# Decayed attention and two MLPs on one core: loads paced by the landing of earlier loads, in place of TensorE products behind instruction-block borders

## The chip, the core and the metric

The kernel runs on one core of one Trainium2 chip. A core has a matrix engine (TensorE, in the profile PE for the products and PEld for the loading of weights into its array), VectorE (DVE), ScalarE (ACT), GpSimd (POOL) and SyncE (SP), which here does nothing but issue transfers. Sixteen DMA engines move the data. The metric is the device time of one execution in microseconds. Before the change it is 558.35 us, the median of three runs (558.33 to 558.46).

## The reference

Three stages follow one another: a blockwise attention with decay over 2 batches, 8 heads, 768 positions and 64 features, then two MLPs over 1536 tokens, 512 features and 2048 hidden features. All of it is in float32.

```python
for b in range(nb):                       # 12 blocks of 64 positions
    qb, kb, vb = (q[:, :, sl], k[:, :, sl], v[:, :, sl])
    intra = einsum('bhic,bhjc->bhij', qb, kb) * Dmask
    intra = einsum('bhij,bhjd->bhid', intra, vb)
    inter = einsum('bhid,bhde->bhie', qb * lam_pow, kv_state)
    out[:, :, sl] = intra + inter
    kv_state = lam_block * kv_state + einsum('bhsd,bhse->bhde', kb * rev_pow, vb)
...
h = x @ w_in;  x = (h * clip(h + 3, 0, 6) / 6) @ w_out      # first MLP
h = x @ w_in2; x = maximum(0.01 * h, h) @ w_out2            # second MLP
```

## The kernel before

**The work.** The attention goes through 12 chunks of 64 positions, both batches at once. For a chunk c, TensorE makes three groups of small float32 products: `scores(c)` (tile `pair`), `state(c)` (tile `a`) and `attn_out(c)` (tile `h`). Around them ScalarE copies the queries (`queries`, L314), the states (`state_copy`, L336) and the high part of the result (`att_x`, L353); VectorE masks the scores (`mask`, L322) and makes the low part (L351); GpSimd decays the keys (`k_decay`, L296). ScalarE and VectorE share the copies of v (`part_v`, L289). The MLPs follow; each weight slice is loaded as `raw`, taken apart by `low_bits` (L416), `magnitude` (L420), `exponent` and `compose`, and split into a high and a low part (`w_high` L445, `w_low` L449), so that a product is three faster ones. The first products of the first MLP (`gemm1(0)`, from the first slice, called w(0,0,0) here) are laid between the last chunks of the attention.

**The loads.** All inputs come through SP's queue, in the order of `LOAD_ORDER` (L47). A chunk's q and k are three loads of 256 KB, the v of two chunks are two loads, and the first weight slices are two loads each. Numbered from 0, load 15 is the last of chunk 3, loads 16 to 18 are chunk 4, 19 and 20 are v of chunks 4 and 5, 21 to 26 are chunks 5 and 6, 27 and 28 v of 6 and 7, 29 to 31 chunk 7, 32 and 33 w(0,0,0), 34 to 36 chunk 8, 37 and 38 v of 8 and 9, 39 to 44 chunks 9 and 10, 45 and 46 v of 10 and 11, 47 and 48 w(0,0,1), 49 to 51 chunk 11. Four buffers hold q and k, three hold v, three hold raw weights.

**The pacing of the loads.** TensorE's program is cut in blocks of 256 instructions, the first border at instruction 193. `mm` counts the instructions and notes the first product at least 8 behind each border. From load 15 on, each group of six loads waits for such a product (`load`, L153 on): loads 15 to 20 for the first border's, 21 to 26 for the second's, and so on.

**The order of the work.** `Order` is a planner. Every operation has engines, a planned duration, a due time, predecessors, and buffers that it takes and frees. `issue` (L69 on) runs a clock of its own, and whenever an engine is free in that clock it issues the ready operation that is due first. Each engine's program is the order in which that happened; on the chip, each engine runs its program strictly in order. The loads take part as operations of one planned engine, "dma" (2.05 for a chunk's three loads, 1.4 for the two of v, 1.45 for a weight slice, and 2.5 more until the data count as there). `in_order` makes each load follow the one before it in `LOAD_ORDER`, and makes the first of a group of six follow the attention product named for it in `AT_BORDER`. These planned times are not times of the chip; they set the order only.

Of the kernel before, what the change touches and what calls it, by code (L numbers as in the profile page):

```python
# [9 lines left out]
F32 = mybir.dt.float32  # L10
# [30 lines left out]
N_DENSE = {("s", 0): 5}  # L41
NQ = 4

FIRST_BORDER, BLOCK, PAST_BORDER = 193, 256, 8
FIRST_LOADS, LOADS_PER_BLOCK = 15, 6
AT_BORDER = (('o', 0), ('o', 1), ('s', 4), ('t', 4), ('o', 5), ('s', 8), ('t', 8), ('o', 9))
LOAD_ORDER = (('qk', 0), ('v', 0), ('qk', 1), ('qk', 2), ('v', 2), ('qk', 3), ('qk', 4), ('v', 4), ('qk', 5), ('qk', 6), ('v', 6), ('qk', 7), (0, 0, 0), ('qk', 8), ('v', 8), ('qk', 9), ('qk', 10), ('v', 10), (0, 0, 1), ('qk', 11))  # L47


class Order:  # L50
# [7 lines left out]
    def add(self, engines, fn, due=1e9, after=(), takes=(), frees=()):  # L58


        engines = [engines] if isinstance(engines, tuple) else engines
        self.ops.append((engines, fn, due, [a for a in after if a is not None], list(takes), list(frees)))
        return len(self.ops) - 1
# [59 lines left out]
def decay_attention_two_mlps(ctx: ExitStack, tc: tile.TileContext, qkk, vv, lam, w1, w2, out):  # L123
    nc = tc.nc
# [13 lines left out]
    od = Order({**sizes, "q": NQ, "pair": 2, **{n: 0 for n in late}, **{f"acc{e}": 0 for e in range(4)}})  # L138
    add = od.add

    def new(n, shape, dtype, name=None):
        return pool[n].tile(shape, dtype, tag=name or n, name=name or n)


    records, borders, loads = [0], [], []

    def mm(out, a, x, **flags):
        at = FIRST_BORDER + BLOCK * len(borders) + PAST_BORDER
        i = nc.tensor.matmul(out, a, x, **flags)  # L149
        if records[0] >= at:  # L150
            borders.append(i.ins)
        records[0] += 4 if a.dtype == F32 else 2

    def load(out, in_):
        i = nc.sync.dma_start(out=out, in_=in_)  # L155
        k = (len(loads) - FIRST_LOADS) // LOADS_PER_BLOCK
        loads.append(i)
        if 0 <= k < len(AT_BORDER):
            tc.add_manual_dep(i.ins, borders[min(k, len(borders) - 1)].name, mybir.DependencyInfo(
                mybir.DependencyClass.Sync, mybir.DependencyReason.DATA), reason="behind the border")  # L160

    starts = [[sum(bs[:i]) for i in range(len(bs) + 1)] for bs in BLOCKS]
    steps = [(l, b, t, f) for l in range(2) for b in range(len(BLOCKS[l])) for t in range(NTT)
# [36 lines left out]
    def dense(n):  # L200

        for i in range(n):
            mm(PA["warm"], zeros[:, :P], zeros.unsqueeze(1).to_broadcast([P, 2, TT // 2]), start=True,
                             stop=True)
# [24 lines left out]
    def lam_rows(_):  # L229

        PA["lam"] = new("h", [P, H], F32)
        mm(PA["lam"], ones, lam_sb, start=True, stop=True)
# [36 lines left out]
    def load_qk(c):  # L269
        def fn(_):  # L270
            for i in (0, 2, 1):
                load(QK[c % NQ][:, i], qkk[c, :, i])
        return fn

    def load_v(c):

        def fn(_):
            vp = new("vs", [P, 2, 2, H, D], F32)
            VS[c], VS[c + 1] = vp[:, 0], vp[:, 1]
            for i in range(2):  # L280
                load(vp[:, i, 0], vv[c + i])
            if c == 0:
                nc.gpsimd.memset(vp[other[1], 0, 1], 0.0)
        return fn
# [15 lines left out]
    def scores(c):  # L300
        def fn(_):

            ps, qk = PA["s", c], QK[c % NQ]
            for h in range(H):
                for b in range(2):
                    mm(ps[own[b], b, h, :], qk[other[b], 1, h, :], qk[other[b], 0, h, :],
                                     start=True, stop=True)
        return fn
# [29 lines left out]
    def attn_out(c):  # L338
        def fn(_):
            ps = PA["o", c] = new("h", [P, KC, 2, C], F32)  # L340
            for b in range(2):
                for h in range(H):
                    mm(ps[own[h % 2], h // 2, b, :], VS[c][:, b, h, :], R[c][:, b, h, :],
                                     start=True, stop=True)
        return fn
# [17 lines left out]
    pieces = {}  # L363
    st, copies, masks, dense_ops, att_ops = {}, {-1: []}, [], [op_warm], []
    for c in range(NSC):
# [5 lines left out]
        s = pieces["s", c] = add(pe, scores(c), d, after=[qc, op_warm])  # L371
# [10 lines left out]
        o = pieces["o", c] = add(pe, attn_out(c), d + 2.6, after=[m, ld["v", c]] + copies[c - 1], takes=["h"])  # L382
        add(("none", 0.0), nothing, after=[o, st.get(c)], frees=["vs"] * (c % 2) + ["r"])
        for n, a in (("s", s), ("t", st.get(c)), ("o", o)):
            i = N_DENSE.get((n, c), 0)
# [17 lines left out]
    def load_w(h):  # L403
        def fn(_):
            l, f, j = h
            RAW[h] = new("raw", [P, DM, 2], U32)
            raw, w = RAW[h].rearrange("p n t -> p (n t)"), (w1, w2)[l][f, j].bitcast(U32)
            for a in (slice(0, DM), slice(DM, 2 * DM)) if l + f < 2 else (slice(0, 2 * DM),):
                (load if h in LOAD_ORDER else nc.sync.dma_start)(raw[:, a], w[:, a])
        return fn  # L410

    def low_bits(h):
        def fn(_):

            CV[h] = [new("cv", [P, DM], U32, "t"), new("cl", [P, DM], U32, "c")]
            nc.scalar.activation(out=CV[h][1], in_=RAW[h][:, :, 0], func=AF.Copy, scale=2.0 ** -29)  # L416
        return fn
# [4 lines left out]
    def exponent(h):  # L422
        def fn(_):
            t = CV[h][0]

            nc.vector.tensor_scalar(out=t.bitcast(F32), in0=t.bitcast(F32), scalar1=MAG_MIN, scalar2=MAG_MAX,  # L426
                                    op0=ALU.max, op1=ALU.min)

            nc.vector.tensor_scalar(out=t, in0=t, scalar1=5, scalar2=2,
                                    op0=ALU.logical_shift_left, op1=ALU.logical_shift_right)  # L430
        return fn
# [22 lines left out]
    def w_sum(l, p, i):  # L454
        def fn(e):
            t1, t2, raw = (x.bitcast(F32) for x in (CV[l, 2 * p, 0][0], CV[l, 2 * p + 1, 0][0], RAW[l, 2 * p + 1, 0]))
            out = raw.rearrange("p n t -> p (n t)").rearrange("p (i n) -> p i n", i=4)
            k1, k2 = slice(0, 2 * P), slice(2 * P, 4 * P)
            a, b, op = ((t2[:, k1], t2[:, k2], ALU.add), (out[:, 0], t1[:, k1], ALU.subtract),
                        (t1[:, k1], t2[:, k1], ALU.subtract), (t1[:, k2], out[:, 1], ALU.subtract))[i]  # L460
            eng[e].tensor_tensor(out=out[:, i], in0=a, in1=b, op=op)
            SB[l, p, "f"] = out
        return fn
# [12 lines left out]
    for l in range(2):  # L476
        for f in range(NF):
            for j in range(2):
                h = (l, f, j)
                held = paired(l, f) and j == 0  # L480
                ld_w = ld[h] = add(("dma", 1.45), load_w(h), takes=["raw"])
                a = add(("act", 0.67), low_bits(h), after=[ld_w], takes=["cv", "cl"])
                m = add(("act", 0.67), magnitude(h), after=[ld_w, a])
                x = add(("dve", 1.2 if h in LOAD_ORDER else 0.85), exponent(h), after=[m])
# [4 lines left out]
            if paired(l, f) and f % 2:  # L489
                p, i = f // 2, None  # L490
                for n in range(4):
                    i = add(("dve", 0.43), w_sum(l, p, n), after=[composed[l, f - 1, 0], composed[l, f, 0], i])
# [3 lines left out]


    def in_order(names):
        n, behind = 0, None
        for h in names:  # L500
            op = ld["vp" if h[0] == "v" else "qk", h[1]] if len(h) == 2 else ld[h]
            k = (n - FIRST_LOADS) // LOADS_PER_BLOCK
            od.ops[op][3].extend(([pieces[AT_BORDER[k]]] if 0 <= k < len(AT_BORDER) else []) + [behind] * (behind is not None))
            n += 3 if h[0] == "qk" else 2
            behind = op
        for h in ld:
            if len(h) == 3 and h not in names:
                od.ops[ld[h]][3].append(behind)

    in_order(LOAD_ORDER)  # L510

    PH, U, G, ACC = {}, {}, {}, {}
# [311 lines left out]
    at = T_FIRST + T_STEP * n1 - 5.44  # L824
# [26 lines left out]
    for s in range(n1 - 2, NS):  # L851
        l, b, t, f = steps[s]
# [304 lines left out]
```

## Time and profile before

| what | us |
|---|---|
| median of the runs | 558.35 |
| the profiled execution, first to last instruction | 559.4 |
| TensorE products busy | 547.4 |
| VectorE busy | 431.6 |
| ScalarE busy | 361.2 |
| attention, until its last product | about 61 |

The profiled execution is 1.05 us longer than the median of the runs, so differences are worked out in the profile and then taken off the median. The page gives each engine's busy time; the table of waits tells, for each engine, what it sat idle for; the timeline lists instructions in order, with the idle time ahead of them; the table of DMA queues counts packets per queue. Queue q8, "instruction", brings TensorE's own instructions; q1 brings the loads.

### The profile page before, as it was taken

The page shows a single profiled execution, that of the slowest core. Times are in us where ns is not written, and L with a number is a line of the kernel's source. Part 1 is how long each engine was busy: PE and PEld are TensorE (multiplying, and loading weights), DVE is VectorE, ACT ScalarE, POOL GpSimd, SP SyncE. Part 2 cuts the span into 40 slices and gives each one's busy share as a digit, 9 for nine tenths or more (in the row PEclk, how much of TensorE's full clock was granted, in tenths as well). Part 3 has the DMA queues.
Part 4 walks back from the last instruction along what each step waited for, and adds up shares of the span by engine and source line. Part 5 has one row for each costly group of instructions (what it writes and reads, how often), then busy time and mean ns, then how long its engine had stood idle before and what let it go on. Part 6 is the DMA issues. An engine that isn't in the chain of part 4 may idle for free.

```text
span 559.4 us, 9243 instructions
## 1 busy us (share of the span) xinstructions
PE 547.4 (98%) x3584; PEld 462.1 (83%) x3584; DVE 431.6 (77%) x718; ACT 361.2 (65%) x634; POOL 59.7 (11%) x68
## 2 busy tenths in 40 slices
PE   8889999999999999999999999999999999999997
PEld 4788888888888888888888888888888888888885
DVE  6769999889898996878879798886467964784342
ACT  4888975668666763588668797587257744573220
POOL 6552001101101101101000000000110100110000
PEclk9999999999999999999999999999999999999999
DMA  8896325237165514334110221332332522411314
GB/s 282 268 328 222 107 87 127 39 98 204 44 164 145 138 24 109 79 110 112 51 65 0 81 108 39 113 117 72 76 76 84 143 75 45 107 43 33 76 44 108
DMA packets 24302, 59.32 MB, mean 106 GB/s; under 512 B 2882, under 2 KB 3138, under 8 KB 24258
## 3 DMA queue, kind: packets, MB, share of 16 engines
q1 hardware_dynamic: 18672, 48.77, 26.6%
q0 software_dynamic: 5184, 9.44, 10.1%
q8 instruction: 28, 0.46, 0.3%
q10 hardware_dynamic: 402, 0.52, 0.3%
q14 instruction: 16, 0.13, 0.1%
HBM read 46.14 MB, written 3.15 MB: 88 GB/s over the span
## 4 chain that ended last, share of the span: by engine, by line
PE 93%; ACT 2%; DMA 2%; issue 1%; DVE 1%; SPq 0%; ACTq 0%
PE acc L149 46%; PE h L149 28%; PE a L149 18%; DMA sums<-qkk 2%; PE pair L149 1%; ACT vs L336 1%; ACT pair L314 1%; DVE kd L251 0%; ACT xh L353 0%; DVE r L322 0%; ACT vs L289 0%; SPq L155 0%; DVE sums L1065 0%; DVE xl L351 0%; ACT t L420 0%
## 5 line engine op out<-in xcount | busy, mean ns | idle before, releaser
L568 POOL DMA_DIRECT2D sums<-st x36 | 31.8, 929 | 424.9 <-ACT st L624 408.0
L149 PE MATMUL acc<-Gh,wh 128*128 128x512 f32 x136 | 53.2, 391 | 0.0
L149 PE MATMUL acc<-Gl,wh 128*128 128x512 f32 x136 | 53.1, 390 | 0.0
L149 PE MATMUL acc<-Gh,wl 128*128 128x512 f32 x136 | 52.9, 389 | 0.0
L149 PE MATMUL acc<-wl,Gh 128*128 128x512 f32 (+1 forms) x128 | 49.6, 387 | 0.0
L149 PE MATMUL acc<-wh,Gh 128*128 128x512 f32 (+1 forms) x128 | 49.6, 387 | 0.0
L149 PE MATMUL acc<-wh,Gl 128*128 128x512 f32 (+1 forms) x128 | 49.4, 386 | 0.0
L416 ACT ACTIVATE c<-raw 128x512 uint32<-128x512 uint32 x64 | 43.0, 674 | 7.7 <-DVE t L439 5.1
L439 DVE CUSTOM_DVE_ANT_0 t<-t,c 128x1024 uint16<-128x1024 uint16 x64 | 44.3, 692 | 2.2
L626 DVE TENSOR_TENSOR sums<-acc,sums 128x512 f32<-128x512 f32 x35 | 24.1, 690 | 28.3 <-PE acc L149 28.1
L437 DVE SCALAR_TENSOR_TENSOR t<-raw,t 128x512 uint32<-128x512 uint32 x64 | 44.8, 700 | 1.0
L449 DVE TENSOR_TENSOR wl<-t,wh 128x512 fp32r<-128x512 f32 (+1 forms) x64 | 42.3, 664 | 3.0 <-ACT wh L445 2.9
L420 ACT ACTIVATE t<-raw 128x512 f32<-128x512 f32 x64 | 42.7, 666 | 0.0
L445 ACT CAST wh<-t 128x512 fp32r<-128x512 f32 (+1 forms) x64 | 37.8, 592 | 3.0 <-PE acc L149 2.3
L149 PE MATMUL h<-xh,s 128*128 128x512 f32 x112 | 38.4, 389 | 0.0
L426 DVE TENSOR_SCALAR t<-t 128x512 f32<-128x512 f32 x64 | 27.7, 433 | 12.9 <-ACT t L420 12.9
L554 DVE TENSOR_TENSOR Gl<-u,Gh 128x512 fp32r<-128x512 f32 x32 | 22.1, 689 | 17.9 <-ACT Gh L751 17.5
L757 ACT ACTIVATE u<-a 128x512 f32<-128x512 f32 x24 | 14.4, 598 | 29.1 <-PE a L149 29.1
L624 ACT COPY st<-acc 128x512 f32<-128x512 f32 x34 | 19.9, 586 | 18.8 <-PE acc L149 16.2
L149 PE MATMUL a<-xh,wl 128*128 128x256 f32 (+1 forms) x92 | 30.7, 333 | 0.0
L149 PE MATMUL a<-xl,wh 128*128 128x256 f32 (+1 forms) x92 | 30.7, 333 | 0.0
L149 PE MATMUL a<-xh,wh 128*128 128x256 f32 (+1 forms) x92 | 30.6, 333 | 0.0
(175 smaller groups left out, 1484.1 us busy)
## 6 DMA issues: line engine op xcount, KB each, us to landing
raw<-w SPq DMA_DIRECT2D x58, 512.0 KB, 3.3
sums<-qkk SPq DMA_DIRECT2D x36, 256.0 KB, 5.2
sums<-st POOLq DMA_DIRECT2D x36, 256.0 KB, 3.8
vs<-vv SPq DMA_DIRECT2D x12, 256.0 KB, 4.7
raw<-w SPq DMA_DIRECT2D x12, 256.0 KB, 4.2
out<-sums SPq DMA_DIRECT2D x19, 128.0 KB, 2.4
out<-sums ACTq DMA_DIRECT2D x3, 128.0 KB, 2.7
out<-sums SPq DMA_DIRECT2D x2, 64.0 KB, 2.3
```

The lines of the kernel that those rows point to most:

```text
L149: i = nc.tensor.matmul(out, a, x, **flags)
L416: nc.scalar.activation(out=CV[h][1], in_=RAW[h][:, :, 0], func=AF.Copy, scale=2.0 ** -29)
L420: return lambda _: nc.scalar.activation(out=CV[h][0].bitcast(F32), in_=RAW[h][:, :, 1].bitcast(F32), func=AF.Abs)
L426: nc.vector.tensor_scalar(out=t.bitcast(F32), in0=t.bitcast(F32), scalar1=MAG_MIN, scalar2=MAG_MAX, op0=ALU.max, op1=ALU.min)
L437: nc.vector.scalar_tensor_tensor(out=t, in0=RAW[h][:, :, 1], scalar=0xC0000000, in1=t, op0=ALU.bitwise_and, op1=ALU.bitwise_or)
L439: nc.vector.tensor_tensor(out=t, in0=t, in1=c, op=ALU.add)
L445: nc.scalar.copy(out=W[h][0][:, cols(*h)], in_=CV[h][0].bitcast(F32)[:, cols(*h)])
L449: return lambda e: eng[e].tensor_tensor(out=W[h][1][:, cols(*h)], in0=CV[h][0].bitcast(F32)[:, cols(*h)], in1=W[h][0].bitcast(F32)[:, cols ...
L554: nc.vector.tensor_tensor(out=gl, in0=U[s], in1=gh.bitcast(F32), op=ALU.subtract)
L568: return lambda _: nc.gpsimd.dma_start(out=SUM[t][:, e, :], in_=STAGE[t, e], accum_op=ALU.add)
L624: nc.scalar.copy(out=STAGE[t, e], in_=ps)
L626: nc.vector.tensor_tensor(out=acc, in0=ps, in1=acc, op=ALU.add)
```

## The change

The counting of instructions, the list of borders and the list `AT_BORDER` go. From load 15 on, each load waits for the landing of the load four places ahead of it in SP's order. All weight loads go through `load` now, the later ones too. In the planner the loads no longer follow any attention product; they follow one another in `LOAD_ORDER` and take their buffers, as before.

```diff
-FIRST_BORDER, BLOCK, PAST_BORDER = 193, 256, 8
-FIRST_LOADS, LOADS_PER_BLOCK = 15, 6
-AT_BORDER = (('o', 0), ('o', 1), ('s', 4), ('t', 4), ('o', 5), ('s', 8), ('t', 8), ('o', 9))
+FIRST_LOADS, IN_FLIGHT = 15, 4
...
-    records, borders, loads = [0], [], []
-
-    def mm(out, a, x, **flags):
-        at = FIRST_BORDER + BLOCK * len(borders) + PAST_BORDER
-        i = nc.tensor.matmul(out, a, x, **flags)
-        if records[0] >= at:
-            borders.append(i.ins)
-        records[0] += 4 if a.dtype == F32 else 2
+    loads = []
+    mm = nc.tensor.matmul
 
     def load(out, in_):
         i = nc.sync.dma_start(out=out, in_=in_)
-        k = (len(loads) - FIRST_LOADS) // LOADS_PER_BLOCK
-        loads.append(i)
-        if 0 <= k < len(AT_BORDER):
-            tc.add_manual_dep(i.ins, borders[min(k, len(borders) - 1)].name, mybir.DependencyInfo(
-                mybir.DependencyClass.Sync, mybir.DependencyReason.DATA), reason="behind the border")
+        loads.append(i.ins)
+        if len(loads) > FIRST_LOADS:
+            tc.add_manual_dep(i.ins, loads[-1 - IN_FLIGHT].name, mybir.DependencyInfo(
+                mybir.DependencyClass.Sync, mybir.DependencyReason.DATA), reason="so many in flight")
...
-                (load if h in LOAD_ORDER else nc.sync.dma_start)(raw[:, a], w[:, a])
+                load(raw[:, a], w[:, a])
...
     def in_order(names):
-        n, behind = 0, None
+        behind = None
         for h in names:
             op = ld["vp" if h[0] == "v" else "qk", h[1]] if len(h) == 2 else ld[h]
-            k = (n - FIRST_LOADS) // LOADS_PER_BLOCK
-            od.ops[op][3].extend(([pieces[AT_BORDER[k]]] if 0 <= k < len(AT_BORDER) else []) + [behind] * (behind is not None))
-            n += 3 if h[0] == "qk" else 2
+            od.ops[op][3].extend([behind] * (behind is not None))
             behind = op
```

## Rows read from the trace of the kernel before

**Rows 1.** Page, part 1: engine, busy us (share of the span), instructions.

```profile
PE 547.4 (98%) x3584; PEld 462.1 (83%) x3584; DVE 431.6 (77%) x718; ACT 361.2 (65%) x634; POOL 59.7 (11%) x68
```

**Rows 2.** Waits of TensorE, whole span: for what, us in total, times, longest.

```profile
PE pair L149 <- issue: 1.9, 2, 1.7
PE a L149 <- issue: 1.4, 2, 1.3
...
PE h L149 <- issue: 0.9, 1, 0.9
PE a L149 <- DVE kd L251: 0.8, 1, 0.8
```

**Rows 3.** Busy time by stretch: start:end, length, each engine's us (instructions), clock, DMA.

```profile
26.00:48.30 22.30, 19.93 (x572) 18.29 (x569) 17.04 (x20) 19.95 (x35) 12.99 (x12) 1.00 0.96 312
...
60.00:300.00 240.00, 239.92 (x1162) 201.30 (x1161) 212.19 (x356) 168.28 (x288) 21.24 (x24) 1.00 0.37 99
```

**Rows 4.** The same view from the start up to three moments.

```profile
0.00:16.80 16.80, 14.55 (x220) 9.43 (x221) 12.18 (x20) 9.15 (x15) 11.70 (x18) 1.00 0.83 282
0.00:22.30 22.30, 19.14 (x343) 13.57 (x343) 17.59 (x25) 14.10 (x24) 14.98 (x20) 1.00 0.87 289
...
0.00:32.60 32.60, 27.49 (x595) 21.45 (x595) 23.68 (x32) 22.44 (x38) 19.56 (x25) 1.00 0.85 286
```

**Rows 5.** Page, part 3: a queue's packets, MB, share of 16 engines.

```profile
q8 instruction: 28, 0.46, 0.3%
```

**Rows 6.** TensorE's timeline: start us, us, instruction [idle before <-releaser].

```profile
20.71 1.15 PE L149 MATMUL h<-r,vs 128*64 128x64 f32 x32
...
23.94 0.97 PE L149 MATMUL pair<-sums 64*64 64x64 f32 x25 [1.70 <-issue]
...
52.14 1.15 PE L149 MATMUL h<-r,vs 128*64 128x64 f32 x32
```

**Rows 7.** DMA queues in 21.4 to 21.6 us, then in 25.1 to 25.3 us.

```profile
q8 instruction: 1, 0.02, 27.4%
...
q8 instruction: 1, 0.02, 33.0%
```

**Rows 8.** SP's timeline: loads issued, from when, over how long.

```profile
7.47 0.96 SPq L155 DMA_DIRECT2D vs<-vv  x2
...
12.88 0.33 SPq L155 DMA_DIRECT2D sums<-qkk  x1
...
17.46 2.71 SPq L155 DMA_DIRECT2D sums<-qkk  x6
...
43.43 44.25 SPq L409 DMA_DIRECT2D raw<-w  x12
```

**Rows 9.** DMA view: 5 to 13 us, then issues at 0.7 and 24.7; us to landing.

```profile
DMA packets 1642, 2.99 MB, mean 373 GB/s; under 512 B 184, under 2 KB 184, under 8 KB 1642
...
vs<-vv SPq DMA_DIRECT2D x2, 256.0 KB, 5.3
...
sums<-qkk SPq DMA_DIRECT2D x1, 256.0 KB, 2.7
...
vs<-vv SPq DMA_DIRECT2D x1, 256.0 KB, 3.3
```

**Rows 10.** Load line L155 and page part 6: issue ns min/median/max; us to landing.

```profile
L155 SPq DMA_DIRECT2D sums<-qkk x36: 327/408/1657, 0.8 to 43.0; - x36
...
raw<-w SPq DMA_DIRECT2D x58, 512.0 KB, 3.3
```

**Rows 11.** Timelines of ScalarE and VectorE: start us, us, instruction [idle before].

```profile
34.12 0.67 ACT L416 ACTIVATE c<-raw 128x512 uint32<-128x512 uint32 x1 [1.65 <-DMA raw<-w]
...
45.40 1.19 ACT L336 COPY vs<-a 64x512 f32<-64x512 f32 x2
...
46.96 0.70 ACT L416 ACTIVATE c<-raw 128x512 uint32<-128x512 uint32 x1
...
37.24 0.42 DVE L289 COPY vs<-vs 64x512 f32<-64x512 f32 x1
```

## The prediction

> **What bounds the kernel now.** I read the page first, then TensorE's waits, then the stretch in which they lie. TensorE is the bound: its products are busy for 547.4 us of the span of 559.4 [rows 1], and from 60 to 300 us for 239.92 of 240 [rows 3]. So a microsecond counts only if TensorE idles less. The table of its waits says where it idles at all: four waits of the attention end on "issue", that is on nothing that the profile shows, and sum to 1.9 + 1.4 + 0.9 = 4.2 us; one more, 0.8, is for VectorE's `kd` [rows 2], which the change does not touch.
>
> The 4.2 us are waits for TensorE's own program. Products and weight loads together are 7168 instructions [rows 1], which is 28 blocks of 256, and queue q8 moved 28 packets [rows 5]. The long wait, 1.70, ends at 23.94 [rows 6]; up to then 686 instructions had run, and up to 32.6, in the wait of 0.9, 1190 [rows 4]. The 504 between are two blocks, but for a few of the sequencer's own that this view leaves out. So TensorE stops at borders. One block is 256 / (572 + 569) x 19.93 = 4.5 us of TensorE's work [rows 3].
>
> The wait depends on what loads are under way. About 441 instructions had run at 16.8 us, so a block began there [rows 4]. The packet with the block behind it starts only between 21.4 and 21.6 [rows 7], 4.7 us later, with six more loads issued from 17.46 on [rows 8]; TensorE resumes 2.5 us after that. The block that begins at 23.94 finds the loads nearly drained, and its packet starts between 25.1 and 25.3, 1.3 us later [rows 7]. That is 1.3 + 2.5 = 3.8 us where little is ahead, so 0.7 less than a block's work: a packet held up by less than 0.7 costs nothing.
>
> **Part 1: at most four loads in flight.** A load of 256 KB at the 373 GB/s of the dense stretch moves in 0.70 us [rows 9]. A lone one lands 2.7 us after its issue, so with four under way mostly one is being moved and the rest are on their way in or being confirmed. A packet of instructions then waits behind 0 to 0.7, which the 0.7 of slack covers. The bounds per border are nothing and 4 x 0.70 - 0.7 = 2.1. I take 0.15, near the lower end, because landings of 5.3 us [rows 9], which show several loads queued, belong to eight in flight. Seven borders lie in the stretch, so 1.0 us stays of 4.2: TensorE gains **3.2 us** if nothing else is late.
>
> **Part 2: the loads' own pace.** Four in flight bring one load each 2.7 / 4 = 0.68 to 3.3 / 4 = 0.83 us [rows 9], and the engines allow 0.70. Issues that meet an instruction packet take up to 1.66 us, where the median is 0.41 [rows 10], so I charge each block 1.1 us without loads: (4.5 - 1.1) / 0.72 = 4.7 loads in 4.5 us. I take 0.9 us a load, with 0.8 and 1.1 as ends. Load 11 is issued at 7.47 and lands some 5.3 later, at 12.8; load 15, which waits for it, is issued at 12.88 today [rows 8, 9]. So it starts as now, lands at 12.9 + 2.7 = 15.6, and load n at 15.6 + 0.9 (n - 15): w(0,0,0) is there at 31.8, v8 (its first half is load 37) at 35.4, w(0,0,1) at 45.3. ScalarE waits 1.65 us for w(0,0,0) until 34.12 now [rows 11]; that wait goes. ScalarE has 19.95 us of work in the 22.3 up to 48.3, as much as TensorE's 19.93 [rows 3], so it needs this to keep up.
>
> **Part 3: the planned order moves.** In the planner the loads no longer wait for the attention products. Going through its clock by hand with the kernel's constants, for the order only, the loads of v6 and w(0,0,0) come 1.45 earlier, v8 1.45, chunk 9 2.3 and w(0,0,1) 2.8. ScalarE's queue is full, so w(0,0,0)'s `low_bits` keeps its place, but VectorE takes `part_v(6)` ahead of `mask(5)` and `part_v(8)` ahead of `mask(7)`; then `compose` of w(0,0,0) is sooner, `w_high(0,0,0)` and `low_bits(0,0,1)` come ahead of `queries(10)`, and `gemm1(0)` ahead of `scores(10)`. The planner counts 0.7 a load and knows nothing of instruction packets, so these operations may stand in an engine's queue before their data land. Behind `low_bits(0,0,1)` on ScalarE stand the copies of `state(8)`, for which `state(9)` and `attn_out(9)` wait. From 45.3: 0.70 for `low_bits`, 1.19 for the copies [rows 11], then three groups of 1.1 on TensorE [rows 6], is 50.5. Today the same work is done when `attn_out(9)` ends, at 52.14 + 1.15 = 53.3 [rows 6]. This path lets through 53.3 - 50.5 = **2.8 us**.
>
> VectorE's wait for v8 is of the same kind: the copy runs at 37.24 [rows 11], with `mask(7)` behind it. At 35.4 it leaves up to 1.8 for what is earlier, and at the ends of the pace 33.2 or 39.8. I charge 0.6 for it, between nothing and 2.6.
>
> **Part 4: what costs nothing.** The added waits are on SP, behind which stand only further loads and, long after, the output's stores. The later weight slices wait too, but for a load that left 4 x 44.25 / 12 = 14.8 us before [rows 8] and needs 3.3 [rows 10]. Counting and borders leave no instruction on the chip. The products stay the same in number.
>
> **Sum.** The gain is the smaller of 3.2 and 2.8, less 0.6: 2.2 us. Behind 60 us TensorE has no idle time [rows 3], so it reaches the end. The profiled span is 1.05 above the median; 558.35 - 2.2 = **556.1 us**.
>
> **The rivals.** *All of it comes back.* Loads at 0.8 or faster put w(0,0,1) at 42.0, no queue waits, and the whole 4.2 goes: 554.1. The lone landing of 2.7 speaks for it; against it stand the long issues [rows 10].
>
> *The fetch does not care.* If an instruction packet is served in turn with the loads, however many are queued, the four waits stay as they are and the time is 558.3; a small gain that the new order eats gives the same. The Trainium skill, "DMA: Bandwidth & Descriptors", section "Queues, rings and completion order", says this: an engine goes round robin between its queues, a packet at a time. By that rule the change wins nothing. The trace disagrees as far as it goes: 4.7 us with many loads, 1.3 with few.
>
> *Slower: the data land behind their place in the queue.* The mechanism is Part 3's wait of ScalarE for w(0,0,1). At 1.1 us a load it lands at 15.6 + 33 x 1.1 = 51.9, and `attn_out(9)` and the rest end at 51.9 + 0.70 + 1.19 + 3.3 = 57.1 in place of 53.3: 3.8 later, 562.1. It decides from a landing at 48.1 on, which is 0.985 us a load. For it speaks that a window of four has no reserve: each 1.1 us lost to an instruction packet is lost for good. Against it, 0.9 is what the rows give.
>
> **How the numbers follow.** The forecast has 0.45 (555 to 557.2), the full gain 0.15, no difference 0.20, slower 0.20. The range 553.8 to 560.5 leaves out the far part of the slower case and a little below the full gain. A measurement of this kernel tells about 0.2%, 1.1 us, from no change; so faster by more is 0.45 + 0.15 = 0.60, within it 0.20, slower 0.20.
>
> **What would show it.** Right: TensorE's waits on "issue" sum to about 1 us in place of 4.2; packets of q8 start within 2 us of a block's beginning; ScalarE's wait for w(0,0,0) is gone and one for w(0,0,1) is new, ahead of the copies of `state(8)`; `gemm1(0)` stands ahead of `scores(10)`; loads 15 to 48 land 0.9 us apart. Wrong: waits on "issue" of 0.7 or more at most borders, which fells Part 1; landings closer than 0.8 or wider than 0.985 apart, which fells Part 2 towards one rival or the other; the old order on ScalarE, which fells Part 3; and new idle time of TensorE behind 60 us, which I exclude.

## The result, and the profile after

The changed kernel takes 566.54 us (four runs, 565.68 to 567.50) against 558.34 us before: a ratio of 1.0147, 95% interval 1.0133 to 1.0162. It is 8.2 us slower; I had forecast 2.2 us faster, and the slower rival ended at 562.1.

What TensorE waited for in the changed kernel, whole span (for what, us in total, times, longest; answers to [rows 2]; a line number is now that of the product's own call):

```profile
PE a L322 <- issue: 3.3, 2, 2.9
PE pair L297 <- DMA sums<-qkk: 1.8, 2, 0.9
PE pair L297 <- ACT pair L305: 1.5, 1, 1.5
PE h L334 <- DVE r L313: 1.3, 1, 1.3
PE pair L297 <- issue: 1.1, 1, 1.1
...
PE h L514 <- DVE ux L735: 0.6, 1, 0.6
PE h L334 <- issue: 0.6, 1, 0.6
PE h L690 <- DVE u L527: 0.6, 1, 0.6
...
PE h L514 <- DVE wl L440: 0.2, 1, 0.2
```

The waits at borders are the three of 0.6, 1.1 and, inside the 3.3, 0.46; they sum to 2.2 us where 4.2 stood. The 2.9 in the first line is no border: the timelines below show that it is for data. Of the second line, 0.84 us is the wait of the first scores for their load, which was 1.18 before. The other entries shown are new, and three of them (0.6, 0.6, 0.2) lie in the MLPs.

The same stretches as [rows 3] (engines PE, PEld, DVE, ACT, POOL, then granted clock, DMA share, GB/s):

```profile
26.00:48.30 22.30, 16.84 (x441) 15.62 (x443) 13.00 (x16) 14.37 (x25) 10.81 (x10) 0.92 0.81 256
60.00:300.00 240.00, 238.55 (x1148) 198.48 (x1145) 210.68 (x355) 166.10 (x286) 21.29 (x24) 1.00 0.38 99
```

Between 26 and 48.3 us the DMA engines moved 256 GB/s where they had moved 312, and every engine did less: TensorE 16.84 us of work where it had done 19.93, ScalarE 14.37 where it had done 19.95.

The chain that ended last, from 2.6 to 50 us (start, us, what), is now nothing but loads:

```profile
12.72 3.74 DMA sums<-qkk
...
16.48 5.01 DMA vs<-vv
...
21.57 4.75 DMA sums<-qkk
...
26.33 4.27 DMA vs<-vv
...
30.62 3.96 DMA raw<-w
...
34.59 3.33 DMA sums<-qkk
...
45.73 4.41 DMA raw<-w
```

Each load in this chain is four places ahead of the next, and each takes 3.3 to 5.0 us from issue to landing. A window of four divides that: load 48, the second half of w(0,0,1), lands at 50.1 where load 15 landed near 15.8, 1.04 us a load. Load 48 is the last line: issued at 45.73, landed 4.41 later.

How this reaches TensorE, in the timelines of ScalarE and VectorE (answers to [rows 11]):

```profile
30.68 0.61 ACT L280 COPY vs<-vs 64x512 f32<-64x512 f32 x1 [3.09 <-DMA vs<-vv]
31.32 1.18 ACT L327 COPY vs<-a 64x512 f32<-64x512 f32 x2
...
35.35 0.68 ACT L407 ACTIVATE c<-raw 128x512 uint32<-128x512 uint32 x1 [1.15 <-DMA raw<-w]
...
50.22 0.67 ACT L407 ACTIVATE c<-raw 128x512 uint32<-128x512 uint32 x1 [3.95 <-DMA raw<-w]
50.91 1.19 ACT L327 COPY vs<-a 64x512 f32<-64x512 f32 x2
...
39.18 0.73 DVE L280 COPY vs<-vs 64x512 f32<-64x512 f32 x1 [4.34 <-DMA vs<-vv]
```

ScalarE stands 3.09 us in its copy of v7, until load 28 lands at 30.6. Behind it are the copies of `state(4)`, which `state(5)` needs; the first ends near 31.9, and TensorE, which has waited 2.87 us, goes on at 32.0. The page puts that wait down to "issue"; the times put it down to load 28. Later ScalarE stands 3.95 us ahead of `low_bits` of w(0,0,1), with the copies of `state(8)` behind it, and VectorE 4.34 us ahead of v8.

The wait of 2.87 costs more than itself. TensorE's timeline around it, then the stretches (columns as above):

```profile
27.98 1.15 PE L297 MATMUL pair<-sums 64*64 64x64 f32 x32
32.00 2.42 PE L322 MATMUL a<-vs,kd 128*64 128x64 f32 x31 [2.87 <-issue]
...
34.27 1.59 PE L334 MATMUL h<-r,vs 128*64 128x64 f32 x31
...
30.00:32.00 2.00, 0.01 (x1) 0.04 (x1) 0.65 (x1) 1.27 (x3) 0.00 (x0) 0.97 0.88 271
32.00:34.00 2.00, 1.89 (x29) 1.70 (x30) 0.99 (x2) 1.94 (x4) 0.00 (x0) 0.50 0.80 261
34.00:36.00 2.00, 2.00 (x46) 1.93 (x46) 0.84 (x1) 0.85 (x2) 1.27 (x2) 0.68 0.88 286
```

From 32 to 34 us the granted clock is 0.50, the lower of the two levels (1.2 GHz), after TensorE had done 0.01 us of work in the two microseconds before. The groups of `state` and `attn_out` take 2.42 and 1.59 us where such groups take 1.15 and 1.10, so the low clock costs 1.27 + 0.49 = 1.8 us.

The sum, trace against trace (565.7 against 559.4, 6.3 us): TensorE is idle for 5.2 us more and busy for 1.0 more. Of the idle time, 3.1 lie between 26 and 48.3 us (5.5 where it was 2.4 [rows 3]), 1.0 in the rest of the attention until 60 us and 1.4 in the MLPs (1.45 where 0.08 stood); up to 26 us it is 0.3 less, the third load having landed 0.8 us sooner. In the busy time the low clock adds 1.8. Against it, the first scores and the five products behind them took 1.15 and 1.25 us here, and 1.97 and 2.10 in the trace of before. The other 0.9 was not traced to one place.

The medians differ by 8.2, not 6.3. In the changed kernel's four executions the time is about 1.8 us above the span (567.5 for a span of 565.7), and so it is in every execution of the kernel before beside the experiments below (1.7 to 1.8). So the execution that I read there, with a span of 559.4, took some 561.2 us, about 2.8 more than the median. What the usual execution has less of is not shown: it can be the waits that I counted on, or the late third load and the slow first products of that trace.

### The profile page after: what moved, and what is told of

Same layout as the page of the kernel before. It is cut to its first block, busy times and chain, and to the rows that moved or that the text cites. A ratio compares the mean times of both kernels' runs of the same rounds, so it can differ in the third digit from the quotient of the medians.

```text
span 565.7 us, 9238 instructions
## 1 busy us (share of the span) xinstructions
PE 548.4 (97%) x3584; PEld 462.6 (82%) x3584; DVE 429.7 (76%) x718; ACT 361.0 (64%) x634; POOL 60.5 (11%) x68
## 4 chain that ended last, share of the span: by engine, by line
PE 84%; DMA 8%; DVE 4%; ACT 1%; issue 1%; SPq 0%; ACTq 0%
PE acc L602 43%; PE h L690 20%; PE a L690 14%; PE h L514 4%; DMA sums<-qkk 3%; DMA vs<-vv 3%; DMA raw<-w 1%; PE a L514 1%; DVE u L527 1%; PE a L602 1%; DVE wl L440 1%; DVE t L428 1%; DVE Gl L540 0%; DVE x_spare L676 0%; DVE t L430 0%
## 5 line engine op out<-in xcount | busy, mean ns | idle before, releaser
L602 PE MATMUL acc<-wl,Gh 128*128 128x512 f32 x124 | 48.4, 391 | 0.0
L602 PE MATMUL acc<-wh,Gh 128*128 128x512 f32 x124 | 48.4, 391 | 0.0
L602 PE MATMUL acc<-wh,Gl 128*128 128x512 f32 x124 | 48.2, 389 | 0.0
L420 DVE TENSOR_SCALAR t<-t 128x512 uint32<-128x512 uint32 x64 | 28.3, 442 | 2.2
L602 PEld LDWEIGHTS acc<-Gh,wl 128*128 128x128 f32 x136 | 25.5, 188 | 5.4
L602 PEld LDWEIGHTS acc<-Gh,wh 128*128 128x128 f32 x136 | 25.6, 188 | 5.2 <-ACT st L613 0.3
```

What stands on the lines that cost most here:

```text
L420: nc.vector.tensor_scalar(out=t, in0=t, scalar1=5, scalar2=2, op0=ALU.logical_shift_left, op1=ALU.logical_shift_right)
L602: mm(ACC[e], a, x, start=(first and n == 0 and not seeded(s, e)), stop=(last and n == 2), skip_group_check=seeded(s, e))
```

## The experiments

Two theories. **Pace:** a window of four brings the loads too slowly, whatever the order. **Order:** the planner, freed of the border operations, puts work in the engines' queues before its data can be there. The first two kernels separate them: one takes the waits of the change with the old plan, the other the plan of the change with the old waits. The first four kernels, the next four and the last three ran on one chip each, beside the kernel before (medians of 559.35, 558.92 and 558.97 us there). The ratios are against those runs, and it is they that are compared with the expectations, which were worked out from 558.3 us. The quotient of two medians lies up to 0.3% off the ratio given; where that matters, the interval decides.

**Old order, four in flight.** The border operations stay in the planner, the loads wait for the fourth before them.

```diff
+AT_BORDER = (('o', 0), ('o', 1), ('s', 4), ('t', 4), ('o', 5), ('s', 8), ('t', 8), ('o', 9))
...
-            od.ops[op][3].extend([behind] * (behind is not None))
+            k = (n - FIRST_LOADS) // LOADS_PER_BLOCK
+            od.ops[op][3].extend(([pieces[AT_BORDER[k]]] if 0 <= k < len(AT_BORDER) else []) + [behind] * (behind is not None))
...
```

> The planner keeps the old order (loads follow the attention products in the plan); at run time each load from the 16th waits for the landing of the load four places ahead. Pace theory (a window of four brings a load only every 1.04 us, as the changed kernel's trace shows: load 15 lands near 15.8, load 48 at 50.1): the loads are as late as in the changed kernel, PE waits for them, 562 to 566 us. Order theory (the loads' pace would do, but the new order puts operations in the engines' queues before their data land): the old order gives them the room, 557 to 560 us, with load 48 again near 50.

Measured: 564.17 us, ratio 1.0102 (1.0070 to 1.0134). The pace alone makes the kernel slower. ScalarE still waits 2.35 us for v7 and 1.93 for w(0,0,1):

```profile
29.65 0.61 ACT L281 COPY vs<-vs 64x512 f32<-64x512 f32 x1 [2.35 <-DMA vs<-vv]
...
49.09 0.67 ACT L408 ACTIVATE c<-raw 128x512 uint32<-128x512 uint32 x1 [1.93 <-DMA raw<-w]
...
60.00:300.00 240.00, 239.93 (x1159) 200.97 (x1158) 211.90 (x357) 166.66 (x285) 21.23 (x24) 1.00 0.38 99
```

The last line, the stretch from 60 to 300 us, shows TensorE without idle time: the 1.4 us in the MLPs are not the pace's. At the borders TensorE does not wait at all in this trace; its one wait on "issue", 1.9 us, ends with the copies behind v7.

**New order, border waits.** The other way round: `mm` and `load` of the kernel before, `in_order` of the changed one.

```diff
...
-            od.ops[op][3].extend(([pieces[AT_BORDER[k]]] if 0 <= k < len(AT_BORDER) else []) + [behind] * (behind is not None))
+            od.ops[op][3].extend([behind] * (behind is not None))
...
```

> The planner's new order, but at run time the loads wait for the products behind the borders as before the change. Pace theory: the loads land as before (load 48 at about 46), so at most the copies of v and low_bits of w(0,0,1) wait a little: 558 to 560.5 us. Order theory: the operations moved ahead wait for v6, v8 and w(0,0,1) nearly as long as in the changed kernel, 562 to 566 us.

Measured: 560.83 us, ratio 1.0033 (1.0013 to 1.0052). The order alone costs 0.3%, and TensorE's waits behind 60 us are there again with it:

```profile
PE h L149 <- DVE ux L744: 0.6, 1, 0.6
PE h L149 <- DVE u L536: 0.6, 1, 0.6
PE h L149 <- DVE wl L449: 0.2, 1, 0.2
```

They are 1.4 of the some 1.8 us that 0.3% is. So the change's 1.47% is about 1.0% of pace and 0.3% of order, which is as near as the intervals tell. VectorE falls behind in the MLPs because operations were issued in another order up front, not because of the loads' pace.

**Six and eight in flight.** One number of the changed kernel, 6 here and 8 in the second.

```diff
-FIRST_LOADS, IN_FLIGHT = 15, 4
+FIRST_LOADS, IN_FLIGHT = 15, 6
```

> The changed kernel with six in flight in place of four. Pace theory: one load each 4.2/6 = 0.70 us plus what the instruction packets take, about 0.8; load 48 lands near 42 to 44, the waits for data go and some waits at borders come back: 556 to 559.5 us. Order theory: still 562 to 566, since the order is that of the changed kernel.

Measured: 560.69 us, ratio 1.0017 (0.9989 to 1.0046). Load 46 lands at 41.3 us, where four in flight brought it at 48.8. Nearly all of the loss is gone with the window, which settles for pace as the larger part.

> The changed kernel with eight in flight, which is also how many loads run before the 16th. Pace theory: loads at 0.7 to 0.8 us each, no waits for data; instruction packets wait behind up to eight loads, so waits on issue of 1 to 2 us at most borders: 557 to 563 us. If packets do not wait behind loads: waits on issue as with four in flight, and 553 to 556 us.

Measured: 562.33 us, ratio 1.0079 (1.0041 to 1.0118). The loads are earlier still (load 46 at 38.1 us), and the waits on "issue" are back, 5.4 us in sum. The first three borders with eight in flight, TensorE's timeline:

```profile
15.85 0.86 PE L334 MATMUL h<-r,vs 128*64 128x64 f32 x22 [0.75 <-issue]
...
21.75 0.97 PE L297 MATMUL pair<-sums 64*64 64x64 f32 x25 [1.58 <-issue]
...
27.13 0.97 PE L322 MATMUL a<-vs,kd 128*64 128x64 f32 x26 [1.01 <-issue]
```

and the same three with four in flight:

```profile
15.67 0.86 PE L334 MATMUL h<-r,vs 128*64 128x64 f32 x22 [0.57 <-issue]
...
21.25 0.97 PE L297 MATMUL pair<-sums 64*64 64x64 f32 x25 [1.15 <-issue]
...
26.09 0.97 PE L322 MATMUL a<-vs,kd 128*64 128x64 f32 x26 [0.46 <-issue]
```

At each of these moments TensorE enters a block, and the packet with the next one is fetched. With eight, these packets start at 19.20, 24.68 and 29.96 us, which is 3.4, 2.9 and 2.8 later; with four at 18.17, 22.99 and 27.51, which is 2.5, 1.7 and 1.4 later. The page of the DMA queues finds them so (18.1 to 18.3 us with four, 19.1 to 19.3 with eight; the share is that of 16 engines):

```profile
q8 instruction: 1, 0.02, 50.9%
...
q8 instruction: 1, 0.02, 32.7%
```

So the packet is late when more loads are queued, as the prediction read it from the trace of before, but not in proportion. With six in flight TensorE enters the same blocks at 15.67, 20.96 and 25.80, and the packets start at 18.22, 23.34 and 29.45, which is 2.6, 2.4 and 3.6 later: as late as with eight.

**Loads alone.** What the window costs with nothing beside it: all computation left out, three stretches of 28 loads.

```diff
+WINDOWS = (4, 6, 8)
...
+                d = nc.sync.dma_start(out=slot, in_=qkk[k // 3 % NSC, :, k % 3])
+                loads.append(d.ins)
+                back = n if i >= n else int(i == 0 and k > 0)
+                if back:
+                    tc.add_manual_dep(d.ins, loads[-1 - back].name, ...
```

> Leaves out the whole computation: 84 loads of 256 KB alone, 28 with four in flight, 28 with six, 28 with eight, each waiting for the landing of the load so many places ahead. TensorE runs nothing, so no packets of its instructions come. Theory A (the window of four is short of the round trip by itself): one load each 0.9 us with four, 0.7 with six and eight. Theory B (it is the instruction packets that stretch it): 0.68 to 0.75 us with four, hardly less with six and eight.

The DMA view in 8 to 24 us (four in flight), 36 to 49 (six) and 62 to 74 (eight): packets and rate, then loads issued and their median us to landing.

```profile
DMA packets 2416, 4.40 MB, mean 275 GB/s; under 512 B 269, under 2 KB 269, under 8 KB 2416
sums<-qkk SPq DMA_DIRECT2D x17, 256.0 KB, 3.9
...
DMA packets 2469, 4.49 MB, mean 345 GB/s; under 512 B 279, under 2 KB 279, under 8 KB 2469
sums<-qkk SPq DMA_DIRECT2D x18, 256.0 KB, 4.5
...
DMA packets 2574, 4.69 MB, mean 391 GB/s; under 512 B 286, under 2 KB 286, under 8 KB 2573
sums<-qkk SPq DMA_DIRECT2D x13, 256.0 KB, 5.4
```

256 KB at 275, 345 and 391 GB/s are 0.95, 0.76 and 0.67 us a load. Theory A holds: the window of four is short by itself, without any instruction packet. A load that shares the queue with three others needs 3.9 us from issue to landing, not the 2.7 of the first one. The rest, from 0.95 to 1.04, I put down to instruction packets, but no run shows it: beside the computation more than these packets is different.

**Old order, six and eight in flight.** If pace and order add up, the old order with six should beat the kernel before; the second run has 8 for 6. The edit is against the old order with four.

```diff
-FIRST_LOADS, LOADS_PER_BLOCK, IN_FLIGHT = 15, 6, 4
+FIRST_LOADS, LOADS_PER_BLOCK, IN_FLIGHT = 15, 6, 6
```

> The planner keeps the old order, six in flight. If the window's cost and the order's cost add up (old order with four: 1.0102; new order with four 1.0147, with six 1.0017), 0.997 to 0.999 of the kernel before: 556.5 to 557.8 us. If the window of six with the old order only brings the waits at borders back: within 0.2% of before. No idle time of TensorE behind 60 us in either case.

Measured: 558.94 us, ratio 1.0004 (0.9988 to 1.0020): the same time, not faster. No idle time behind 60 us, as expected; the waits on "issue" sum to 5.7 us in its trace, and one of 1.8 us came in that the page puts down to ScalarE's copy of v. It stands at a border, and is one of those waits too, as the last experiment explains: 7.5 us in sum.

> The planner keeps the old order, eight in flight, so nothing but buffers paces the loads. If instruction packets wait behind the loads ahead of them, waits on issue of 5 to 6 us in sum: 559 to 561 us. If packets are served in turn with the loads, the waits on issue stay near those of four in flight (2.2 us): 555 to 557 us.

Measured: 559.53 us, ratio 1.0023 (1.0003 to 1.0044), with 6.2 us of waits on "issue". Nothing paces these loads but the buffers and a limit of eight, which the loads before the 16th keep too (in the changed kernel, load 10 is issued at 5.94, when load 2 has landed at 5.92). The kernel loses only 0.2% against the one with borders. So making the loads wait for the borders, as the kernel before does, is worth little, and a window that is wide enough costs no more than that.

**A plan that knows the pace.** If the order hurts because the plan takes 0.7 us a load, telling it the real figure should help.

```diff
-        ld["qk", c] = add(("dma", 2.05), load_qk(c), d, takes=["q"])
+        ld["qk", c] = add(("dma", 3.1), load_qk(c), d, takes=["q"])
...
```

> The changed kernel, four in flight, with the planner told about 1.03 us for a load in place of 0.7 (3.1 for three loads, 2.1 for two). Theory that the new order hurts because the plan places operations ahead of their data: ScalarE's wait for w(0,0,1) (3.95 us) and VectorE's for v8 (4.3) go, and the time is at or below that of the old order with four, 560 to 564 us. Theory that the pace alone sets the time: 565 to 567, with the waits moved elsewhere.

Measured with four in flight: 563.86 us, ratio 1.0088 (1.0053 to 1.0122). ScalarE no longer waits for w(0,0,1) at all, nor VectorE for v8, and the MLPs have no idle time; 0.9% stays. It is what the old order with four costs, so this fits the order's share once more, in the other direction. The waits that stay have moved: ScalarE waits 4.6 us for v in sum, and TensorE stands still for 2.8 us until 43.7.

**The changed kernel again**, beside the last two.

> The changed kernel as it is, beside the next two. Additive theory: the window of four costs 1.0% (old order with four), the new order 0.3% (new order with the border waits), so 1.013 to 1.016 of the kernel before. A theory in which the order costs nothing and only the window counts: 1.009 to 1.011.

Measured: 568.09 us, ratio 1.0176 (1.0133 to 1.0218), on another chip than the first time. That is above the 1.013 to 1.016 expected, which the interval still reaches; the window alone, 1.009 to 1.011, it does not reach. ScalarE waits 2.45 us for v7, 0.80 for w(0,0,0) and 3.81 for w(0,0,1), as before. TensorE has one wait on "issue" in the whole span:

```profile
PE a L322 <- issue: 2.0, 1, 2.0
```

It ends at 30.92, when the first of the two copies that stand behind v7 is done (they run from 30.24 to 31.42). So the waits at borders, 2.2 us in the first trace of this kernel, are all gone in this one, and the kernel is as slow.

**Six in flight with a plan for six.**

```diff
-        ld["qk", c] = add(("dma", 2.05), load_qk(c), d, takes=["q"])
+        ld["qk", c] = add(("dma", 2.4), load_qk(c), d, takes=["q"])
...
```

> Six in flight, and the planner told 0.8 us a load (2.4 for three, 1.6 for two), which is what six in flight give. If the idle time behind 60 us (1.4 us in every kernel with the new order) comes from the plan that thinks loads faster than they are, it goes, and the time is 0.997 to 1.000 of before. If any order but the old one brings such idle time, 1.001 to 1.004.

Measured: 562.38 us, ratio 1.0068 (1.0046 to 1.0091). A miss: at 0.8 us a load in the plan, the three waits in the MLPs (0.6, 0.6, 0.2) are there still, and the waits on "issue" are no less than with the uncorrected plan (5.5 us against 4.6, and 0.9 more there at a border under another name). That the plan runs ahead of the loads is therefore not the whole reason of the order's cost. Which difference of the order sets VectorE back in the MLPs was not tried; the plan told 1.03 us a load has another order again, and no such idle time.

**Borders and six in flight.** The kernel before with a second wait, for the landing of the load six places ahead.

```diff
...
+        if len(loads) > FIRST_LOADS:
+            tc.add_manual_dep(i.ins, loads[-1 - IN_FLIGHT].ins.name, mybir.DependencyInfo(
+                mybir.DependencyClass.Sync, mybir.DependencyReason.DATA), reason="so many in flight")
```

> The kernel before with both waits: behind the borders, and for the landing of the load six places ahead. If an instruction packet waits behind the loads that are queued when it is asked for, the packet of the second border (4.7 us behind it in the kernel before, with six loads issued within 2.7 us) starts within 3 us, the wait of 1.7 us falls below 1, and the time is 0.996 to 0.999 of before. If packets do not care about queued loads, the waits on issue stay at 4.2 us and the time at 0.999 to 1.002.

Measured: 559.51 us, ratio 0.9994 (0.9973 to 1.0015): no difference that can be told. The second border's packet starts between 18.5 and 18.7 us, and TensorE's timeline has

```profile
15.41 0.86 PE L149 MATMUL h<-r,vs 128*64 128x64 f32 x22 [0.31 <-issue]
20.97 0.97 PE L149 MATMUL pair<-sums 64*64 64x64 f32 x25 [0.88 <-issue]
```

so the packet comes 3.2 us behind the start of its block where it came 4.7 behind (3 was expected), and the wait is 0.88 where it was 1.70. What that saves is lost at the borders behind it. One of them hides under another name; ScalarE's timeline, then TensorE's:

```profile
33.13 1.20 ACT L317 COPY pair<-sums 64x512 f32<-64x512 f32 x2
...
36.29 1.15 PE L149 MATMUL pair<-sums 64*64 64x64 f32 x32 [1.54 <-ACT vs L339]
```

These scores need the copies of the queries, which were done at 34.33, and not the copy at L339 that the page names. They stand behind the 1441st of TensorE's products and weight loads. In the traces with such waits they come there, or behind the 437th, 687th, 939th, 1191st, 1693rd and 1945th or within four of it, which are the borders, and each ends 1.3 to 1.6 us after a packet of instructions has been moved (here one from 33.04, which took 1.88). Counted so, the waits at borders sum to 4.6 us here and to 4.2 before, which is why the time stays. Where the loads wait for the borders and the order is new, they are 5.1. Where the loads only wait for the landing of others, they are 5.5 to 7.5 in the three traces with six in flight, 5.8 and 6.8 with eight. With four they are 2.2 in the first trace of the changed kernel and nothing in its second, with the old order, and with the plan that knows the pace. No version beat the kernel before.

## Why the prediction was wrong, step by step

**The bound** was read rightly: TensorE's idle time decides, and the four waits on "issue" are for its own instructions.

**Part 1, the waits at borders,** was right in its mechanism, and its size lies between two traces. Of 4.2 us, 1.0 was to stay; 2.2 stayed in the first trace and nothing in the second. So this part of the gain came, and the kernel lost 8.2 us all the same. In the first trace the packets start sooner, but at two of the three borders TensorE resumes 3.1 us after the packet's start (18.17 to 21.25, 22.99 to 26.09), not 2.5: these two packets took 1.6 and 1.7 us to move, where those that the prediction read took 0.9 and 1.1. It is not the four loads as such, since with the old order and four in flight the packets of the same borders took 1.0; the cause is open. Besides, the execution that I read was slower than the usual one by about 2.8 us, so the base may have been too large.

**Part 2, the loads' own pace, is the step that failed.** I took the landing of the first, lone load, 2.7 us, and divided by four. What counts is the time that a load needs among three others, and that is 3.9 us, as the loads alone show: 0.95 us a load by their rate and not 0.68 to 0.83. The charge for instruction packets was too high in turn: from 0.95 to 1.04, if all of it is theirs, is 0.4 us a block (4.5 / 0.95 = 4.7 loads against 4.5 / 1.04 = 4.3, at 0.95 us each), not 1.1. The two errors nearly made up for each other, and by luck: 4.7 loads in 4.5 us are 0.96 us a load. But I then took 0.9, which does not follow from that sum. At 0.96, load 48 would have been due at 47.3, 0.8 us ahead of the 48.1 from which the slower rival decides; the pace was 1.04 and it landed at 50.1. The end of 1.1 that I gave was on the right side of it.

**Part 3, the order,** was right in the mechanism, place and reach of the wait for w(0,0,1). `part_v(8)`, `low_bits(0,0,1)` and `gemm1(0)` stand where the hand reading of the planner put them, and ScalarE's new wait is ahead of the copies of `state(8)`. With load 48's real landing at 50.1 the path gives 50.1 + 0.70 + 1.19 + 3.3 = 55.3; in the trace the same work ends at 54.43 + 1.15 = 55.6. What it missed is the wait for v7, which is in the old order as well: load 28 lands at 30.6, and I had not followed `part_v(7)` at all. At 15.6 + 13 x 0.9 = 27.3 it would have mattered little. ScalarE's wait for w(0,0,0) was to go and shrank only from 1.65 to 1.15 us. And v8 was charged with 0.6: VectorE starts its copy at 39.18, near the late end of 39.8, after 4.34 us of waiting; what that alone costs TensorE was not separated.

**Part 4** put the rest at nothing, and new idle time behind 60 us was excluded. It is there, 1.4 us, with every kernel that has the change's order, and with none that has the old one. A plan that is altered in the first 50 us alters what is issued long after; "the products stay the same in number" says nothing on that.

**The rivals.** The slower one is what happened: it decides from 0.985 us a load on, and the pace was 1.04. It was given 0.20. Its price was too small because it stopped at one path: at its place it would have cost 2 us; the low clock (1.8), the wait for v7 and the MLPs came on top. The rival that the fetch does not care is refuted as far as these runs go: at the first three borders packets start 2.8 to 3.4 us late with eight in flight and 1.4 to 2.5 with four, and the waits at borders fell with four alone. Why six are no better than eight stays open. The page "DMA: Bandwidth & Descriptors" of the Trainium skill, section "Queues, rings and completion order", by whose rule of taking turns the queue's length should not matter, differs from that; the measurement decides.

**Range and chances.** The upper end of 560.5 left out half of the slower case, whose own figure was 562.1. A case with a mechanism, a place and a decision point within a tenth of the value taken (0.985 against 0.9) deserved more than 0.20, and its whole reach in the range.

## What to carry to other kernels

A window of n transfers brings one per n-th of the time that a transfer takes among n, so measure it there: the first transfer, with nothing ahead of it, is faster (2.7 us here, against 3.9 among four). A wait that holds loads back also holds back everything that an in-order queue has put behind their use. Here TensorE stood still for 2.9 us for it, and the lower clock behind that made the loss larger by 1.8. Where a planner's order hangs on the same constants as the waits, test the two apart: here they cost 1.0% and 0.3%, and the second shows for the most part far behind the altered loads, at 84, 130 and 137 us.

## What the runs showed of the hardware that I had not expected

A 256 KB load lands 2.7 us after its issue when it is the first, and 3.9, 4.5 and 5.4 us after with four, six and eight under way; the rates are 275, 345 and 391 GB/s. TensorE's granted clock fell to 0.50 for more than 3 us after a standstill of 2.9 us, which cost 1.8 us; it was 0.50 from 32 to 34 us, too, after standstills of 2.05 us in the second trace of the changed kernel and 1.94 with the old order and four. A packet of instructions, 16 KB, took 0.9 to 1.1 us to move in most cases and up to 2.5, and at the borders where TensorE waited it went on 1.3 to 1.6 us after the packet's end. With the old order and nothing but eight in flight as pacing, the kernel lost only 0.2%.
